# Softmax probabilities copied by a DMA into fp32r buffers before their transposes; seven entries of the ordering list changed

## The chip, the cores and the metric

The kernel runs as one program on one core of a Trainium2 chip. Its engines are TensorE (PE, matrix products and transposes), VectorE (DVE), ScalarE (ACT), GpSimd (POOL) and SyncE (SP), which only issues DMA transfers here. The metric is the device time of one execution in microseconds (us).

## The reference

Clustered attention over 16 heads (2 batches of 8), then two feed-forward blocks. Per head q, k and v are 768x64; the result is 1536x512.

```python
mask = q_assign[:, :, :, None] == k_assign[:, :, None, :]   # argmax over 16 centroids each
scores = np.where(mask, scale * q @ k.T, -1e9)
attn = np.exp(scores - scores.max(-1))
attn = attn / (attn.sum(-1) + 1e-9)
x = (attn @ v)                                # -> (1536, 512)
x = ((x @ w1) * (x @ w2)) @ w3 @ w_out        # first block, d_ff 1024
h = x @ w_in                                  # second block, d_ff 2048
out = (h * np.clip(h + 3, 0, 6) / 6) @ w_out2
```

## The kernel before

Products are made in fp32r, with each operand split into a rounded high part and a remainder (`hi`, `lo`), so that one product is three or four passes. The feed-forward weights come as 64-bit numbers and are made into fp32 by ACT, POOL and DVE (`conv_ops`, lines 665 to 707, tiles raw, cvt, cvs).

One head is worked in six row blocks c of 128 queries. For each block `scores` (L495) makes 128x768 scores into one of two PSUM slots of `pst`; `smax` (L504, DVE) takes the negated row maximum; `sexp` (L512, ACT) writes the exponentials as one fp32 tile p and sums them. Three blocks make a half `hf`. For each of the six key blocks of a half, `p_T` (L520) transposes three 128x128 pieces of the three p tiles into a PSUM tile `ptr`, with the fp32 identity `id_f`; `p_hi` (ACT) copies it rounded into `ph`, `p_lo` (DVE) writes the remainder into `pl`; after two key blocks `av` (L540) multiplies both with v. So there are 32 halves, 192 groups of three transposes, 96 score blocks. The stacked q and k are transposed the same way in `stack_T` (L363), but from fp32r tiles (`qs`, `ks`) with the fp32r identity `id_r`.

While attention runs, PE also does the product w3 @ w_out (`psw`, L771), and later x @ w1 and x @ w2 of the first batch (`psab`, L843). When the last head is done, its memory is opened for the next stage (`open_top`), where `psx` (L956) begins, and from there the second block follows (`psab` L1093, `psh` L1403, `po` L1447).

The order on every engine is fixed before the run. Each step is entered with `op(name, engine, duration, function, needs, due, take, drop, lat)`: `take` and `drop` name rings of buffers of limited number, `lat` is added to the end of a transfer. `Plan.order` (L64) places the steps one after another by these durations, choosing on each engine among those that can start soonest the one with the lowest `due`; in attention one unit of `due` is one score block. Every engine, SP included, then works through its own list in that order and waits at an instruction whose inputs are not there. All transfers are issued by SP. `attn_ops` (L613) enters the steps of a head: S1 and S are the two parts of the scores, mx the maximum, ex the exponential, pT, ph, pl, av the rest. `LT` sets how many units after the first block of a half its transposes are due.

Of the kernel before, what the change touches and what calls it, by code (L numbers as in the profile page):

```python
# [8 lines left out]
F32 = mybir.dt.float32  # L9
# [127 lines left out]
def cluster_attention_moe_kernel(  # L137
# [14 lines left out]
    nc = tc.nc  # L152
# [42 lines left out]
    def blk(i):  # L195
# [14 lines left out]

    NQ, NK, NP, NO = 1, 1, 6, 1
    plan = Plan({
        "raw": 2, "rawx": 6, "cvt": 2, "cvs": 2, "hl": 2, "wT": 3, "m": 1, "s": 3, "r": 2, "a": 1, "x": 1, "x1b": 1,
        "qn": 2, "kn": 2, "vn": 1, "qs": NQ, "ks": NK, "vs": 2, "qB": 2, "kB": 2, "qA": 2, "kA": 2, "oh": NO,
        "p": NP, "ph": 2, "pl": 2, "den": 2, "T": 1, "O": 1, "rdb": 1, "as1": 1, "as2": 1, "asb": 2, "rdr": 1,
        "ga": 1, "gb": 1, "w16": 1, "whl": 1, "gA": 1, "gB": 1, "gv": 2, "t": 6, "h": 1, "gh": 6, "sn": 5, "L": 2, "bL": 2, "bs": 8, "F": 1, "wof": 2,
    })
    op = plan.op  # L220
# [203 lines left out]
    def prep_ops(h):  # L424
# [26 lines left out]
        for hf in range(2):  # L451
# [7 lines left out]
        op(("pa", h), "pe", 1.3, lambda: assign_mm(h), [("CqB", h, 0), ("CqB", h, 1), ("CkB", h, 0), ("CkB", h, 1),  # L459
            ("cTc", 1)] + [("pa", h - 1)] * (h > 0),  # L460
           due=b - 5, take=("s",))
        for n in range(8):
# [7 lines left out]
    def flat(t):  # L470
        return t.rearrange("p a f -> p (a f)")

    pps, dens, psS, phl, avs, Ts, rdb, ptr = {}, {}, {}, {}, {}, {}, {}, {}


    psr = ps_r.tile([128, 2, S], F32, tag="r", name="pst")
# [30 lines left out]

    def sexp(h, c):
        d = dens[h]
        p = at.tile([128, 2, HF], F32, tag="p", name="p", bufs=NP)  # L510
        n = NC * h + c
        done["ex", n] = [other_banks(nc.scalar.activation(  # L512
            out=flat(p), in_=psS.pop((h, c)), func=AF.Exp, bias=d[:, 0, c:c + 1], accum_out=d[:, 1, c:c + 1]
        ), ("S", n + 1))]
        pps[h, c] = flat(p)
# [88 lines left out]
    def pair_lo(e, pr):  # L604
        sub_on(e, xT0[0][:, 1, pr, :], flat(Ts.pop(pr)), xT0[0][:, 0, pr, :])

    LT, LA = 3.4, 1.6

    def attn_ops(h):
        b = NC * h  # L610
        for c in range(NC):
            t = b + c
            nd = [("C" + n, h, f) for n in ("qB", "kB", "k") for f in range(2)] + [("Cq", h, c // 3)]  # L613
            last = c == NC - 1
            prev = [("ex",) + divmod(t - 1, NC)] if t else []
            nd += [("S1",) + divmod(t - 1, NC)] if t else []
            nd += [("ex",) + divmod(t - 2, NC)] if t > 1 else []
            op(("S1", h, c), "pe", 0.43, lambda c=c: scores(h, c, 0), nd, due=t, take=("r",))
            op(("S", h, c), "pe", 0.22, lambda c=c: scores(h, c, 1), [("S1", h, c)] + prev, due=t + 0.1,
               drop=("qB", "kB", "qA", "kA") if last else ())  # L620
# [3 lines left out]
            op(("ex", h, c), "act", 0.88, lambda c=c: sexp(h, c), (("mx", h, c),), due=t + 0.6, take=("p",),  # L624
                drop=("r",))
        for hf in range(2):
            for s in range(3):
                u = b + 3 * hf + s + LT
                for i in range(2):
                    op(("pT", h, hf, s, i), "pe", 0.325, lambda hf=hf, s=s, i=i: p_T(h, hf, s, i),  # L630
                       [("ex", h, 3 * hf + c) for c in range(3)], due=u + 0.2 * i, take=("s",),
                       drop=("p",) * 3 if s == 2 and i == 1 else ())
# [5 lines left out]
                op(("av", h, hf, s), "pe", 0.65, lambda hf=hf, s=s: av(h, hf, s),  # L638
                   [("pl", h, hf, s, 0), ("pl", h, hf, s, 1), ("vlo", h)] + [("av", h, hf, s - 1)] * (s > 0),
                       due=u + LA,  # L640
                   take=("a",) if s == 0 else (), drop=("ph",) + (("vs",) if hf and s == 2 else ()))
# [153 lines left out]
    for hf in range(2):  # L795
        for m in range(J1):
# [9 lines left out]
                drop=("s",))  # L806
            for kk in range(4):
                g, fin = 4 * hf + kk, m == J1 - 1
                op(("w", m, g), "pe", 0.645, lambda m=m, g=g: w_mm(m, g),
                   [("wtl", m, hf), ("wol", g)] + ([("w", m, g - 1)] if kk else [("w", m - 1, 4 * hf + 3)] if m else  # L810
                                                   [("w", J1 - 1, 3)] if hf else []),
                   due=wdue(m, g), take=("m",) if kk == 0 else (),
                   drop=(("wT",) if kk == 3 else ()) + (("hl", ("ga", "gb")[hf]) if fin and kk == 3 else ()) + (
                       ("x1b",) if fin and g == J1 - 1 else ()))
# [45 lines left out]
    for j in range(J1):  # L860
# [9 lines left out]
        for hf in range(2):  # L870
            for w in range(2):
                u = j + (2 * hf + w) / 4
                d = AB0 + AR * u
                for kk in range(KD):
                    op(("ab", j, hf, w, kk), "pe", 0.485, lambda j=j, hf=hf, w=w, kk=kk: ab_mm(j, hf, w, kk),
                       [("abl", j, w), ("xl", kk)] + ([("ab", j, hf, w, kk - 1)] if kk else []),
                       due=d + AR * kk / 16, take=("m",) if kk == 0 else (),
                       drop=("hl",) if hf and w and kk == KD - 1 else ())
# [676 lines left out]
```

## Time and profile before

| | |
|---|---|
| time, median of 3 runs | 786.79 us (786.77 to 787.0) |
| profiled execution, first to last instruction (its span) | 785.5 us; what lies around the span is not in the page: 1.3 us by the median |
| PE busy | 762.6 us (97%) |
| DVE busy | 659.7 us (84%) |
| ACT busy | 534.7 us (68%) |
| POOL busy | 258.2 us (33%) |
| granted TensorE clock | 0.997 of 2.4 GHz, mean |
| DMA moved | 94.24 MB, mean 120 GB/s |

An engine's busy time counts its instructions; a PE instruction is counted until its modelled end, while the next one already starts, so the time that an instruction costs is read from the start of one to the start of the next. The profile names idle time by what ended it. A row is line, engine, operation, tiles, and the count.

### The profile page before, as it was taken

The numbers are of one execution on the slowest core, as the hardware profiler recorded it, in microseconds if no ns is written. First come the engines' busy times: TensorE is split into PE (matmuls) and PEld (weight loads), VectorE is DVE, ScalarE is ACT, GpSimd is POOL, SyncE is SP. The second block draws the span as 40 slices with busy tenths as digits, with TensorE's granted clock in tenths as the row PEclk, the third lists the DMA queues.
The fourth block names the chain that finished last, engine by engine and source line by source line (L and its number), as shares of the span: only waits on it lengthen the run. The fifth ranks groups of instructions, "written<-read, shape, count | busy, mean of one in ns | idle before, by whom it ended". The sixth has DMA issues, their size and how long they took to land.

```text
span 785.5 us, 12835 instructions
## 1 busy us (share of the span) xinstructions
PE 762.6 (97%) x4471; PEld 698.3 (89%) x4471; DVE 659.7 (84%) x1193; ACT 534.7 (68%) x1061; POOL 258.2 (33%) x277
## 2 busy tenths in 40 slices
PE   6799999999999999999999999999999999999997
PEld 5688887789899999999999999989898989888986
DVE  7998898999999897788998798979999976666742
ACT  5679897777877786767763565746776667555543
POOL 5733757344555454323232131611122111010100
PEclk9999999999999999999999999999999999999999
DMA  7443343333454441333344543366533424212102
GB/s 248 131 149 105 89 138 101 109 113 97 120 159 146 114 148 53 90 112 114 106 138 132 152 160 114 109 217 213 164 124 120 138 91 148 81 55 68 41 14 81
DMA packets 57041, 94.24 MB, mean 120 GB/s; under 512 B 5168, under 2 KB 33936, under 8 KB 56976
## 3 DMA queue, kind: packets, MB, share of 16 engines
q1 hardware_dynamic: 56976, 93.43, 38.4%
q8 instruction: 35, 0.57, 0.3%
q14 instruction: 30, 0.25, 0.1%
HBM read 71.34 MB, written 15.78 MB: 111 GB/s over the span
## 4 chain that ended last, share of the span: by engine, by line
PE 83%; DVE 9%; ACT 4%; issue 3%; DMA 1%; ACTq 0%; POOL 0%; DVEq 0%; SPq 0%; POOLq 0%
PE po L1447 17%; PE psh L1403 15%; PE psab L843 8%; PE pst L495 7%; PE av L540 7%; PE psab L1093 7%; PE ptr L520 7%; PE psw L771 5%; PE psx L956 4%; PE pa L389 3%; DVE den L504 1%; DVE pl L184 1%; DVE cvs L720 1%; ACT p L512 1%; PE ptkB L363 1%
## 5 line engine op out<-in xcount | busy, mean ns | idle before, releaser
L711 POOL TENSOR_SCALAR cvt<-cvt 128x512 f32<-128x512 f32 x72 | 75.8, 1056 | 192.6 <-ACT cvt L187 181.2
L187 ACT ACTIVATE ph<-ptr 128x384 fp32r<-128x384 f32 x192 | 91.0, 487 | 44.9 <-PE ptr L520 43.9
L184 DVE TENSOR_TENSOR pl<-ptr,ph 128x384 fp32r<-128x384 f32 x192 | 103.4, 550 | 16.9 <-ACT ph L187 15.3
L504 DVE TENSOR_REDUCE den<-pst 128x1 f32<-128x768 f32 x96 | 91.2, 950 | 8.6 <-PE pst L495 7.0
L512 ACT ACTIVATE p<-pst,den 128x768 f32<-128x768 f32 x96 | 86.3, 898 | 9.8 <-DVE den L504 9.0
L520 PE MATMUL ptr<-id_f,p 128*128 128x128 f32 x576 | 88.4, 274 | 1.7 <-DVE pl L184 1.0
L843 PE MATMUL psab<-xT,abhl 128*128 128x384 f32 x384 | 86.9, 349 | 0.6 <-ACT asb L187 0.6
L520 PEld LDWEIGHTS ptr<-id_f,p 128*128 128x128 f32 x576 | 68.6, 140 | 11.4 <-DVE pl L184 2.3
L495 PE MATMUL pst<-kB,qB 128*128 128x512 f32 x192 | 70.1, 368 | 4.4 <-ACT p L512 4.1
L540 PE MATMUL av<-ph,vs 128*128 128x384 f32 x192 | 69.7, 363 | 0.0
L843 PEld LDWEIGHTS psab<-xT,abhl 128*128 128x128 f32 x384 | 64.4, 189 | 2.9 <-ACT asb L187 1.1
L540 PE MATMUL av<-pl,vs 128*128 128x384 f32 x192 | 65.0, 339 | 0.0
L495 PE MATMUL pst<-kA,qA 128*128 128x512 f32 x192 | 63.9, 338 | 0.2 <-issue 0.2
L187 ACT ACTIVATE m_sn<-psh 128x384 f32<-128x384 f32 x64 | 31.1, 486 | 36.1 <-PE psh L1403 35.9
L1425 ACT ACTIVATE tt<-m_sn,three 128x384 f32<-128x384 f32 x48 | 29.5, 617 | 37.3 <-DVE m_sn L1413 28.2
L724 DVE SCALAR_TENSOR_TENSOR cvs<-cvt,cvs 128x512 int32<-128x512 int32 x72 | 52.4, 731 | 0.2
L771 PE MATMUL psw<-woh,wT 128*128 128x512 f32 x128 | 52.6, 417 | 0.0
L187 ACT ACTIVATE cvt<-raw 128x512 f32<-128x512 f32 x72 | 47.6, 666 | 6.9 <-DVE m_gB L184 3.5
L720 DVE SCALAR_TENSOR_TENSOR cvs<-raw,cvs 128x512 int32<-128x512 int32 x72 | 49.6, 694 | 0.4
L495 PEld LDWEIGHTS pst<-kB,qB 128*128 128x128 f32 x192 | 36.1, 188 | 10.1 <-ACT p L512 7.7
L716 DVE TENSOR_SCALAR cvs<-cvt 128x512 int32<-128x512 int32 x72 | 33.5, 470 | 12.2 <-POOL cvt L711 6.7
L1447 PE MATMUL po<-m_hl,m_gv 128*128 128x512 f32 x162 | 43.7, 393 | 0.0
(203 smaller groups left out, 1948.9 us busy)
## 6 DMA issues: line engine op xcount, KB each, us to landing
raw<-in_moe_w_dram SPq DMA_DIRECT2D x32, 512.0 KB, 3.8
m_gb<-set SPq DMA_DIRECT2D x64, 256.0 KB, 3.2
raw<-in_moe_w_out_dram SPq DMA_DIRECT2D x24, 512.0 KB, 3.9
raw<-in_moe_w_in_dram SPq DMA_DIRECT2D x16, 512.0 KB, 4.0
set<-cvs SPq DMA_DIRECT2D x32, 256.0 KB, 3.8
abp<-cvs SPq DMA_DIRECT2D x16, 256.0 KB, 2.2
b_gv<-abp SPq DMA_DIRECT2D x16, 256.0 KB, 2.8
qn<-in_q_dram SPq DMA_DIRECT2D x16, 192.0 KB, 4.1
```

What stands on the lines that cost most here:

```text
L184: nc.vector.tensor_tensor(out=out, in0=a, in1=b, op=ALU.subtract)
L187: nc.scalar.activation(out=out, in_=in_, func=AF.Copy, **kw)
L495: x = mm(out=psr[:, t, ks_], lhsT=TT["q" + nm, h][:, i, cs_], rhs=flat(TT["k" + nm, h])[:, ks_], start=st, stop=sp)
L504: done["mx", n] = [other_banks(nc.vector.tensor_reduce(out=dens[h][:, 0, c:c + 1], in_=psS[h, c], axis=AX.X, op=ALU.max, negate=True), ("S ...
L512: done["ex", n] = [other_banks(nc.scalar.activation(out=flat(p), in_=psS.pop((h, c)), func=AF.Exp, bias=d[:, 0, c:c + 1], accum_out=d[:, 1 ...
L520: nc.tensor.transpose(pt[:, blk(c)], pps[h, 3 * hf + c][:, blk(2 * s + i)], id_f)
L540: mm(out=t[:, 0:HF], lhsT=vs_t[h][:, 2 * s + i, :], rhs=x_[:, i, :], start=(s == 0 and i == 0 and n == 0), stop=(s == 2 and i == 1 and n = ...
L711: (nc.gpsimd.tensor_scalar if e == "pool" else ts)(out=tf, in0=tf, scalar1=H_MAX, scalar2=-H_MAX, op0=ALU.min, op1=ALU.max)
L771: mm(out=ps, lhsT=wT[m, hf][:, a, blk(kk)], rhs=w_[hf][:, kk, :], start=(kk == 0 and n == 0), stop=(kk == 3 and n == 2))
L843: mm(out=ps[:, 0:HF], lhsT=s[:, w, a, blk(kk)], rhs=xT0[0][:, x_, kk, hf * HF:hf * HF + HF], start=(kk == 0 and n == 0), stop=(kk == KD - ...
L1403: mm(out=ps[:, 0:HF], lhsT=left(p, l, a, kk), rhs=x[:, x_, kk, :], start=(st and kk == 0 and m == 0), stop=(kk == 1 and m == 2), skip_grou ...
L1447: mm(out=outs[b, c], lhsT=g[:, a, blk(c % 3)], rhs=w[:, w_, :], start=(first and a == 0 and w_ == 0), stop=(last and a == 1))
```

## The change

Each p tile is now written under the name `praw` into a ring of three fp32 buffers. A new step `pd` has SP copy it (128 partitions x 3 KB, 384 KB) into an fp32r tile of the old ring `p` of six, bit for bit. The transposes read that tile with `id_r` and write an fp32r PSUM tile, which `p_hi` and `p_lo` read as fp32, as before. They now need the three copies of a half in place of the three exponentials.

```diff
+        "p": NP, "pr": NX, ...                       # NX = 3, NP = 6
...
     def sexp(h, c):
-        p = at.tile([128, 2, HF], F32, tag="p", name="p", bufs=NP)
+        p = praw[h, c] = at.tile([128, 2, HF], F32, tag="pr", name="praw", bufs=NX)
...
+    def p_hop(h, c):
+        t = at.tile([128, 2, HF], F32R, tag="p", name="p", bufs=NP)
+        nc.sync.dma_start(out=t.bitcast(F32), in_=praw.pop((h, c)))
+        pps[h, c] = flat(t)
...
-        pt = ptr[i] = ps_s.tile([128, 512], F32, tag="s", name="ptr")
+        pt = ptr[i] = ps_s.tile([128, 512], F32R, tag="s", name="ptr")
-            nc.tensor.transpose(pt[:, blk(c)], pps[h, 3 * hf + c][:, blk(2 * s + i)], id_f)
-        phl[h, hf, s, i, "t"] = pt
+            nc.tensor.transpose(pt[:, blk(c)], pps[h, 3 * hf + c][:, blk(2 * s + i)], id_r)
+        phl[h, hf, s, i, "t"] = pt.bitcast(F32)
...
-    LT, LA = 3.4, 1.6
+    LT, LA = 4.2, 1.6
...
-            op(("ex", h, c), "act", 0.88, ..., due=t + 0.6, take=("p",), drop=("r",))
+            op(("ex", h, c), "act", 0.88, ..., due=t + 0.6, take=("pr",), drop=("r",))
+            op(("pd", h, c), "dma", 1.3, lambda c=c: p_hop(h, c), (("ex", h, c),), due=t + 0.7, take=("p",),
+                drop=("pr",), lat=2.2)
...
-                    op(("pT", h, hf, s, i), "pe", 0.325, ..., [("ex", h, 3 * hf + c) for c in range(3)], ...)
+                    op(("pT", h, hf, s, i), "pe", 0.18, ..., [("pd", h, 3 * hf + c) for c in range(3)], ...)
...
-                op(("w", m, g), "pe", 0.645, ...)
+                op(("w", m, g), "pe", 0.695, ...)
```

The other entries: `pa` 1.3 to 1.35, `S1` 0.43 to 0.47, `S` 0.22 to 0.238, `av` 0.65 to 0.70, `ab` 0.485 to 0.525. All instructions after L216 stand up to six lines lower.

The lists on the engines change from the first head on. First, PE in the last half of the last head, from its last score product (`pst` 128x256) to the first transposes of that half (`ptr`, three or six in a row). The order before:

```order
L495 MATMUL pst<-kA,qA 128x256
L520 MATMUL ptr<-id_f,p 128x128 x3
L843 MATMUL psab<-xT_1204,abhl 128x384 x6
L520 MATMUL ptr<-id_f,p 128x128 x3
L843 MATMUL psab<-xT_1204,abhl 128x384 x3
L540 MATMUL av<-ph,vs 128x384
L540 MATMUL av<-pl,vs 128x384
L540 MATMUL av<-ph,vs 128x384
L540 MATMUL av<-pl,vs 128x384
L843 MATMUL psab<-xT_1204,abhl 128x384 x3
L520 MATMUL ptr<-id_f,p 128x128 x6
```

Here the earlier `ptr` rows belong to the half before, and the last row is the first of the last half. The order now, from the rows that follow the last score product, a group of three `ptr`, three `psab`, three `ptr` and six `psab`:

```order
L544 MATMUL av<-ph,vs 128x384
L544 MATMUL av<-pl,vs 128x384
L544 MATMUL av<-ph,vs 128x384
L544 MATMUL av<-pl,vs 128x384
L849 MATMUL psab<-xT_1291,abhl 128x384 x3
L524 MATMUL ptr<-id_r,p 128x128 x6
L544 MATMUL av<-ph,vs 128x384
L544 MATMUL av<-pl,vs 128x384
L544 MATMUL av<-ph,vs 128x384
L544 MATMUL av<-pl,vs 128x384
L849 MATMUL psab<-xT_1291,abhl 128x384 x9
L524 MATMUL ptr<-id_r,p 128x128 x3
```

Six more transposes of the half before, a further `av` and six more `psab` now stand ahead of the first transposes of the last half.

Second, SP while the sixth to eighth head runs (`qA`, `kA`: stacked q and k moved to other partitions; `vn`: v of a head; `abp`: converted weights stored; numbers are those of buffers). The order before:

```order
L588 DMA rdb_2567<-rd7_117 64x768
L692 DMA raw_2849<-in_moe_w1_dram 128x4x256
L836 DMA abp0_86<-cvs_2773 128x512
L329 DMA vn_2956<-in_v_dram 128x384
L692 DMA raw_3022<-in_moe_w2_dram 128x4x256
L373 DMA qA_131<-qB_3002 64x768
L836 DMA abp0_86<-cvs_2924 128x512
L373 DMA kA_133<-kB_3039 64x768
```

The order now, from the same `rdb` on:

```order
L592 DMA rdb_2624<-rd7_117 64x768
L698 DMA raw_2937<-in_moe_w1_dram 128x4x256
L518 DMA p_2968<-praw_2950 128x768
L518 DMA p_3006<-praw_2992 128x768
L842 DMA abp0_86<-cvs_2858 128x512
L329 DMA vn_3062<-in_v_dram 128x384
L518 DMA p_3079<-praw_3053 128x768
L518 DMA p_3123<-praw_3100 128x768
L373 DMA qA_131<-qB_3098 64x768
L373 DMA kA_133<-kB_3121 64x768
L698 DMA raw_3173<-in_moe_w2_dram 128x4x256
L518 DMA p_3194<-praw_3153 128x768
```

The copies stand between the loads and stores, each behind whatever the row above it waits for.

Third, PE at the end of attention, up to the first `psx`. The order before:

```order
L520 MATMUL ptr<-id_f,p 128x128 x6
L843 MATMUL psab<-xT_1204,abhl 128x384 x3
L540 MATMUL av<-ph,vs 128x384
L540 MATMUL av<-pl,vs 128x384
L540 MATMUL av<-ph,vs 128x384
L540 MATMUL av<-pl,vs 128x384
L540 MATMUL av<-ph,vs 128x384
L540 MATMUL av<-pl,vs 128x384
L540 MATMUL av<-ph,vs 128x384
L540 MATMUL av<-pl,vs 128x384
L843 MATMUL psab<-xT_1204,abhl 128x384 x24
L956 MATMUL psx_5427<-gh_5389,Whl 128x384 x18
```

And now:

```order
L524 MATMUL ptr<-id_r,p 128x128 x6
L544 MATMUL av<-ph,vs 128x384
L544 MATMUL av<-pl,vs 128x384
L544 MATMUL av<-ph,vs 128x384
L544 MATMUL av<-pl,vs 128x384
L849 MATMUL psab<-xT_1291,abhl 128x384 x12
L544 MATMUL av<-ph,vs 128x384
L544 MATMUL av<-pl,vs 128x384
L544 MATMUL av<-ph,vs 128x384
L544 MATMUL av<-pl,vs 128x384
L849 MATMUL psab<-xT_1291,abhl 128x384 x12
L962 MATMUL psx_5611<-gh_5586,Whl 128x384 x18
```

Twelve `psab` moved from behind the last `av` to before it; twelve are left between the last `av` and the first `psx`.

## Rows read from the trace of the kernel before

**Rows 1.** The page: the chain that ended last, shares of the span by line.

```profile
PE po L1447 17%; PE psh L1403 15%; PE psab L843 8%; PE pst L495 7%; PE av L540 7%; PE psab L1093 7%; PE ptr L520 7%; PE psw L771 5%; PE psx L956 4%; PE pa L389 3%; DVE den L504 1%; DVE pl L184 1%; DVE cvs L720 1%; ACT p L512 1%; PE ptkB L363 1%
```

**Rows 2.** Busy time by stretch: length, PE, PEld, DVE, ACT, POOL, clock, DMA, GB/s.

```profile
40.00:400.00 360.00, 354.55 (x2355) 323.33 (x2354) 323.75 (x609) 282.78 (x610) 161.73 (x182) 1.00 0.39 117
160.00:240.00 80.00, 78.84 (x529) 70.67 (x528) 76.71 (x147) 64.50 (x140) 37.88 (x44) 1.00 0.40 119
```

**Rows 3.** Groups by line and shape: busy us, mean ns, idle before.

```profile
L520 PE MATMUL ptr<-id_f,p 128*128 128x128 f32 x576 | 88.4, 274 | 1.7 <-DVE pl L184 1.0 <-ACT qA L187 0.2
...
L363 PE MATMUL ptkB<-id_r,ks 128*128 128x128 f32 x96 | 13.1, 249 | 0.1
```

**Rows 4.** Timeline of PE around both kinds of transposes: start, length.

```profile
228.79 0.37 PE L363 MATMUL ptqB<-id_r,qs 128*128 128x128 f32 x3
229.00 1.28 PE L843 MATMUL psab<-xT,abhl 128*128 128x384 f32 x6
230.12 0.28 PE L495 MATMUL pst<-kB,qB 128*128 128x256 f32 x1
230.23 0.28 PE L495 MATMUL pst<-kA,qA 128*128 128x256 f32 x1
230.35 0.82 PE L520 MATMUL ptr<-id_f,p 128*128 128x128 f32 x6
230.93 0.42 PE L540 MATMUL av<-ph,vs 128*128 128x384 f32 x1
231.19 0.33 PE L540 MATMUL av<-pl,vs 128*128 128x384 f32 x1
231.36 0.34 PE L540 MATMUL av<-ph,vs 128*128 128x384 f32 x1
...
231.71 0.40 PE L495 MATMUL pst<-kB,qB 128*128 128x512 f32 x1
231.94 0.40 PE L495 MATMUL pst<-kA,qA 128*128 128x512 f32 x1
```

**Rows 5.** Timeline: third block of one half, scores to transposes.

```profile
249.78 0.28 PE L495 MATMUL pst<-kA,qA 128*128 128x256 f32 x1
...
251.47 0.90 ACT L512 ACTIVATE p<-pst,den 128x768 f32<-128x768 f32 x1
...
253.42 0.49 PE L520 MATMUL ptr<-id_f,p 128*128 128x128 f32 x3
```

**Rows 6.** Timeline: the same of the last half of the last head.

```profile
380.40 0.28 PE L495 MATMUL pst<-kA,qA 128*128 128x256 f32 x1
...
383.00 0.89 ACT L512 ACTIVATE p<-pst,den 128x768 f32<-128x768 f32 x1
...
383.99 0.82 PE L520 MATMUL ptr<-id_f,p 128*128 128x128 f32 x6
```

**Rows 7.** Line 373, 192 KB between SBUF tiles: issue to landing.

```profile
DMA to landing us min/median/max: 2.6/2.8/4.8
```

**Rows 8.** Line 692, 512 KB loads: issue to landing.

```profile
DMA to landing us min/median/max: 3.3/3.9/8.3
```

**Rows 9.** The page's DMA queue over the span.

```profile
q1 hardware_dynamic: 56976, 93.43, 38.4%
```

**Rows 10.** What SP's queue waited for, 20 to 400 us: total, times, longest.

```profile
SPq L692 <- DVE cvs L720: 83.4, 31, 7.8
SPq L329 <- POOL vs L181: 64.7, 13, 9.0
```

**Rows 11.** Timeline: last products of attention, and psx.

```profile
394.43 0.44 PE L540 MATMUL av<-pl,vs 128*128 128x384 f32 x1
394.89 2.38 PE L843 MATMUL psab<-xT,abhl 128*128 128x384 f32 x12
...
397.85 2.35 PE L843 MATMUL psab<-xT,abhl 128*128 128x384 f32 x12 [0.58 <-ACT asb L187]
...
400.04 4.15 PE L956 MATMUL psx<-gh,Whl 128*128 128x384 f32 x23
```

More of the change, by code (lines that the diff above doesn't have):

```diff
@@ L206, in cluster_attention_moe_kernel @@
     rd_dram = [tc.dram_tile([NC, 128], F32, name=f"rd{h}") for h in range(NH)]
-    NQ, NK, NP, NO = 1, 1, 6, 1
+    NQ, NK, NP, NO, NX = 1, 1, 6, 1, 3
     plan = Plan({
@@ L216, in cluster_attention_moe_kernel @@
         "qn": 2, "kn": 2, "vn": 1, "qs": NQ, "ks": NK, "vs": 2, "qB": 2, "kB": 2, "qA": 2, "kA": 2, "oh": NO,
-        "p": NP, "ph": 2, "pl": 2, "den": 2, "T": 1, "O": 1, "rdb": 1, "as1": 1, "as2": 1, "asb": 2, "rdr": 1,
+        "p": NP, "pr": NX, "ph": 2, "pl": 2, "den": 2, "T": 1, "O": 1, "rdb": 1, "as1": 1, "as2": 1, "asb": 2, "rdr": 1,
         "ga": 1, "gb": 1, "w16": 1, "whl": 1, "gA": 1, "gB": 1, "gv": 2, "t": 6, "h": 1, "gh": 6, "sn": 5, "L": 2, "bL": 2, "bs": 8, "F": 1, "wof": 2,
@@ L458, in prep_ops @@
                 (("Ck", h, hf), ("Dq", h)), due=dd + 0.06, drop=("s",))
-        op(("pa", h), "pe", 1.3, lambda: assign_mm(h), [("CqB", h, 0), ("CqB", h, 1), ("CkB", h, 0), ("CkB", h, 1),
+        op(("pa", h), "pe", 1.35, lambda: assign_mm(h), [("CqB", h, 0), ("CqB", h, 1), ("CkB", h, 0), ("CkB", h, 1),
             ("cTc", 1)] + [("pa", h - 1)] * (h > 0),
@@ L471, in flat @@
         return t.rearrange("p a f -> p (a f)")
-    pps, dens, psS, phl, avs, Ts, rdb, ptr = {}, {}, {}, {}, {}, {}, {}, {}
+    praw, pps, dens, psS, phl, avs, Ts, rdb, ptr = {}, {}, {}, {}, {}, {}, {}, {}, {}
     psr = ps_r.tile([128, 2, S], F32, tag="r", name="pst")
@@ L617, in attn_ops @@
             nd += [("ex",) + divmod(t - 2, NC)] if t > 1 else []
-            op(("S1", h, c), "pe", 0.43, lambda c=c: scores(h, c, 0), nd, due=t, take=("r",))
-            op(("S", h, c), "pe", 0.22, lambda c=c: scores(h, c, 1), [("S1", h, c)] + prev, due=t + 0.1,
+            op(("S1", h, c), "pe", 0.47, lambda c=c: scores(h, c, 0), nd, due=t, take=("r",))
+            op(("S", h, c), "pe", 0.238, lambda c=c: scores(h, c, 1), [("S1", h, c)] + prev, due=t + 0.1,
                drop=("qB", "kB", "qA", "kA") if last else ())
@@ L623, in attn_ops @@
                take=("den",) if c == 0 else ())
-            op(("ex", h, c), "act", 0.88, lambda c=c: sexp(h, c), (("mx", h, c),), due=t + 0.6, take=("p",),
+            op(("ex", h, c), "act", 0.88, lambda c=c: sexp(h, c), (("mx", h, c),), due=t + 0.6, take=("pr",),
                 drop=("r",))
+            op(("pd", h, c), "dma", 1.3, lambda c=c: p_hop(h, c), (("ex", h, c),), due=t + 0.7, take=("p",),
+                drop=("pr",), lat=2.2)
         for hf in range(2):
@@ L629, in attn_ops @@
                 for i in range(2):
-                    op(("pT", h, hf, s, i), "pe", 0.325, lambda hf=hf, s=s, i=i: p_T(h, hf, s, i),
-                       [("ex", h, 3 * hf + c) for c in range(3)], due=u + 0.2 * i, take=("s",),
+                    op(("pT", h, hf, s, i), "pe", 0.18, lambda hf=hf, s=s, i=i: p_T(h, hf, s, i),
+                       [("pd", h, 3 * hf + c) for c in range(3)], due=u + 0.2 * i, take=("s",),
                        drop=("p",) * 3 if s == 2 and i == 1 else ())
@@ L637, in attn_ops @@
                        (("ph", h, hf, s, i),), due=u + 0.2 * i + 0.2, drop=("s",))
-                op(("av", h, hf, s), "pe", 0.65, lambda hf=hf, s=s: av(h, hf, s),
+                op(("av", h, hf, s), "pe", 0.70, lambda hf=hf, s=s: av(h, hf, s),
                    [("pl", h, hf, s, 0), ("pl", h, hf, s, 1), ("vlo", h)] + [("av", h, hf, s - 1)] * (s > 0),
@@ L808, in cluster_attention_moe_kernel @@
                 g, fin = 4 * hf + kk, m == J1 - 1
-                op(("w", m, g), "pe", 0.645, lambda m=m, g=g: w_mm(m, g),
+                op(("w", m, g), "pe", 0.695, lambda m=m, g=g: w_mm(m, g),
                    [("wtl", m, hf), ("wol", g)] + ([("w", m, g - 1)] if kk else [("w", m - 1, 4 * hf + 3)] if m else
@@ L874, in cluster_attention_moe_kernel @@
                 for kk in range(KD):
-                    op(("ab", j, hf, w, kk), "pe", 0.485, lambda j=j, hf=hf, w=w, kk=kk: ab_mm(j, hf, w, kk),
+                    op(("ab", j, hf, w, kk), "pe", 0.525, lambda j=j, hf=hf, w=w, kk=kk: ab_mm(j, hf, w, kk),
                        [("abl", j, w), ("xl", kk)] + ([("ab", j, hf, w, kk - 1)] if kk else []),
```

1 line of the change is left out of this document (removed).

## Prediction

> **What bounds the kernel now.** I read the chain that ended last first: the reader is to see that nearly all its large shares are TensorE lines, those of attention (pst, av, ptr, psab L843, psw, pa) and those after it, while VectorE and ScalarE come in with one per cent a line [rows 1]. Then the busy time by stretch. Between 40 and 400 us, where the changed steps run, TensorE is busy 354.55 of 360 us and VectorE 323.75; in the tightest part, 160 to 240, they are busy 78.84 and 76.71 of 80 [rows 2]. So TensorE bounds attention, and VectorE stands so close behind it that it can take over. The stages after 400 start from the end of attention, through psx [rows 11]; what attention gains or loses therefore moves the end by about as much. Last I read the timeline for what an operation costs from start to start, since the durations of TensorE overlap.
>
> **What the transposes give.** In the group view the 576 fp32 transposes take 88.4 us of TensorE, 0.153 each; the fp32r transposes of the stacked k, same shape and same kind of operands as the new ones, take 13.1 for 96, 0.136 each [rows 3]. By that the change saves 576 x 0.017 = 9.8 us. The timeline gives a second value [rows 4]. Six fp32 transposes start at 230.35 and the next product at 230.93, 0.58; that product then runs 0.26 to the next start where its like takes 0.17 (231.19 to 231.36), so 0.09 more of the cost lies on it: 0.67 for six, 0.335 for three. Three fp32r transposes take 0.21 (228.79 to 229.00), and the six products behind them 1.12, which is 0.1 over six at 0.17: 0.29 to 0.31 for three. The saving by this is about 0.04 a group, 192 x 0.04 = 7.7 us. I take the middle, 0.045 a group, 8.6 us. The list's own step, 0.325 to 0.18, would be 0.145 x 192 = 27.8 us, and nothing in the trace bears the 0.18 out.
>
> It matters here that fp32 is not slow in this place. A product of 512 columns takes 0.23 from start to start (231.71 to 231.94), one fp32 transpose of 128 columns 0.58/6 = 0.097 [rows 4]; four passes over 128 columns would have cost about the former. The Trainium skill (TensorE: Matmul & The Clock Gate, Terms) says that a load or product carries a transpose mode that is four times faster for fp32; by that rule the fast form is already in use before the change and little is left to gain. The trace agrees: 0.097 against 0.07. Read without that rule, as fp32 at a quarter of the rate, the change would be worth 576 x (0.23 - 0.07) = 92 us, which the trace rules out, since the whole group takes 88.4.
>
> **What the copy costs.** 96 copies of 384 KB are added, issued by SP. The trace has no such transfer. Its neighbours on both sides are the 192 KB moves between SBUF tiles, which land 2.6 us after their issue at best and 2.8 in the median, and the 512 KB loads, 3.3 and 3.9 [rows 7, 8]. By size 384 KB stands at 0.6 between them: 3.0 at best, 3.5 in the median. The ends for the range are 2.6 and 4.8, the longest of the 192 KB moves. The bytes: 93.43 MB took 38.4% of the span on the 16 engines [rows 9], so 37.7 MB more take 122 us of all of them, and the share in attention goes from 0.39 to about 0.7. The DMA engines stay below full, but a copy will meet a load in front of it more often than a load does now. I take 3.7 us.
>
> What does it collide with? The wait of the transposes moves from the exponential to the copy. From the start of a third block's last score product to the end of its exponential the trace shows 2.6 us in one half (249.78 to 252.37) and 3.5 in the last (380.40 to 383.89); TensorE had 3.6 us of other work in between in both (253.42 and 383.99 are the first transposes), which left 1.05 and 0.10 [rows 5, 6]. This work is what covers the copy. In the new order, for the last half, it is 12 transposes, 21 products psab, 8 av and the score product: 4 x 0.295 + 21 x 0.175 + 8 x 0.17 + 0.12 = 6.3 us, 2.7 more than before. I added up the rows of all 32 halves so, at 0.17 to 0.19 for a product of 384 columns, 0.23 for 512, 0.11 for 256 and 0.1 for a transpose [rows 4]: the cover grows by 3.5 us in the median, to 7.7, with some six halves at 5 to 6.4. Against a copy of 3.7 the typical half keeps its margin, and the short ones are late: the last by 3.5 + 3.7 - 6.3 = 0.9 us, with the shorter exponential path of [rows 5] nothing. I put 4 to 5 us on all short halves together: six at about 0.7. Behind a late transpose stand, on TensorE, the av products and the next scores, for which VectorE (mx) and ScalarE (ex) wait. The bounds are 0 (copies at 3.0) and, with copies at 4.8, about 23 us by the same covers and a mean path of 3.2.
>
> The Trainium skill (DMA: Bandwidth & Descriptors, Anatomy of one DMA) puts a transfer at about 2.0 us fixed plus its bytes at 436 GB/s; an estimate by that page is 2.0 + 0.9 = 2.9 us for a copy. The fit is for another way of issuing, and the 192 KB moves at 2.8 [rows 7] are above the 2.5 that it gives for them. By it no half would be late and the sum would be the whole 8.6 us.
>
> **The queue.** SP works in order. Before, it stood 64.7 us at loads of q, k and v until GpSimd had freed a buffer, 9.0 at the longest, and 83.4 at weight loads until VectorE had [rows 10]. Nothing urgent stood behind them. Now copies do: in the second order a load of v stands ahead of two copies. Each list is drawn up with these waits in it, so I add nothing of its own for it, but it is where the landing time can grow beyond 4 us.
>
> **Other edits.** praw has three buffers and a block comes each 3.8 us (96 in some 360), so a buffer is free long before ScalarE wants it: nothing. The copies, the maxima and the remainders on VectorE stay the same in number and size: nothing. The six raised durations remove no instruction; the list gets nearer the trace for products, and further off for the transposes (0.18 for what costs 0.295, 192 x 0.115 = 22 us too little). I take nothing for the reordering, with 3 us on either side. At the end of attention 24 psab (4.7 us) covered what lies between the last av and psx, with 0.58 us of waiting in it (394.89 to 400.04) [rows 11]; now 12 do, 2.1 us. The path there is a PSUM copy, a copy of the gate and a subtraction; before, the first psx could start 5.2 us after, and a stall of up to 1 us may come in place of the 0.58: I add 0.4.
>
> **Sum.** 8.6 saved, less 4.3 for late copies and 0.4 at the end: 3.9 us. On the profiled span of 785.5 that is 781.6; the median of the runs is 1.3 above the span, so 782.9.
>
> **The rivals.** First, the copies come late and it is slower. The mechanism is the copy for the third block of each half, held by SP's order or by a load in front. It decides from the point where late halves cost 8.6 us, by the covers above at a landing of about 4.1 us; at 4.5, 14 us are lost and the time is 786.8 + 5.4 = 792, at 4.8 it is 801. For it: the margin of 0.10 [rows 6], a DMA share going to 0.7, loads that took up to 8.3 us [rows 8]. Against: the median of everything near in size is below 4, and most halves have more cover than need.
>
> Second, VectorE takes the gain. It is busy 96% between 160 and 240 [rows 2], its work in attention is not less, and what TensorE saves turns into waits for pl and mx. Time 786 to 787. Against: over 40 to 400 it has 36 us idle, four times the saving.
>
> Third, the list is right about 0.18: 27.8 us off TensorE. VectorE's 36 us of idle would then be nearly used up, and I give it half, 773. Against it stand all of [rows 3, 4].
>
> **Chances.** Forecast 0.52, with a range of its own of 778 to 786; late copies 0.27; VectorE 0.16; the cheap transposes 0.05. The time is 782.9. The range for 8 in 10 goes from 775 (part of the third case, reordering in our favour) to 797 (most of the first). What measurement can tell here is about 0.2%, 1.6 us. Faster by more: 0.54, from the forecast less its upper edge, the third case, and a little of the second. Within: 0.18. Slower: 0.28, the first case and a little of the second.
>
> **What would show it.** In the profile after: fp32r transposes at about 0.21 for three from start to start and near 78 us for the 576; copies landing at 3.5 to 4 us; TensorE's idle time ahead of ptr, now 1.7 us, at some 5 with the DMA p<-praw named; the first psx near 396 and the same distance from there to the end. Copies at 4.5 or more with tens of us of waiting ahead of ptr would prove the first rival; no such wait and psx still at 400, the second; transposes at 0.18 or less with their follower, the third.

## Result and profile after

The changed kernel takes 798.31 us (median of 4 runs, 797.01 to 801.13), the kernel before beside it 786.89: the ratio is 1.0135, 95% interval 1.0112 to 1.0158. It is 11.4 us slower; 3.9 us faster was forecast. The profiled execution has a span of 799.3 us, 13.8 above that of before; it is the longest of the four, 801.13.

Busy time by stretch of the changed kernel (columns: the stretch, its length, busy us and count of TensorE, of its weight loads, of VectorE, ScalarE and GpSimd, then the granted clock, the DMA share and GB/s). The second and third row answer to [rows 2]; the first runs from 20 us to the first psx:

```profile
core 0: us, PE busy (x) PEld busy (x) DVE busy (x) ACT busy (x) POOL busy (x), PEclk, DMA share, GB/s
20.00:412.56 392.56, 370.74 (x2446) 332.33 (x2445) 344.83 (x632) 294.78 (x634) 176.19 (x203) 0.98 0.62 206
40.00:400.00 360.00, 344.82 (x2292) 310.19 (x2291) 318.13 (x588) 275.36 (x595) 156.94 (x183) 0.98 0.63 210
160.00:240.00 80.00, 76.69 (x522) 66.34 (x522) 72.67 (x137) 62.04 (x136) 36.06 (x43) 1.00 0.61 203
95.00:100.00 5.00, 3.78 (x18) 3.20 (x19) 4.51 (x5) 2.05 (x5) 4.45 (x4) 0.73 0.63 182
100.00:105.00 5.00, 5.00 (x23) 4.50 (x24) 2.31 (x6) 2.35 (x5) 1.79 (x3) 0.58 0.42 130
145.00:150.00 5.00, 5.00 (x22) 4.71 (x22) 4.42 (x7) 0.87 (x2) 4.02 (x5) 0.51 0.64 192
150.00:155.00 5.00, 4.25 (x25) 3.69 (x25) 4.10 (x9) 3.41 (x8) 0.80 (x2) 0.81 0.42 141
```

The stretch from 20 us to the first psx in the kernel before:

```profile
20.00:400.04 380.04, 370.61 (x2444) 335.43 (x2443) 342.16 (x636) 295.69 (x637) 177.60 (x201) 1.00 0.40 118
```

The two first rows hold the result. The same work up to psx takes 392.56 us instead of 380.04. TensorE's idle time went from 9.4 to 21.8 (length less busy). Its busy time did not fall, though the transposes became cheaper: the granted clock was below 1.0 in some stretches, down to about 0.5, its 1.2 GHz level. Counted in stretches of 5 us as (1 - clock) x 5, that is 8.5 us of full-speed work; 370.74 - 8.5 = 362.2 is 8.4 below before. VectorE and ScalarE had hardly more to do than before (344.83 and 294.78 against 342.16 and 295.69). They and TensorE waited for each other.

Where the time goes is read from the start of one step in both traces: the exponentials of the 7th, the 37th and the last of the 96 blocks, before and now.

```profile
47.30 0.91 ACT L512 ACTIVATE p<-pst,den 128x768 f32<-128x768 f32 x1
156.15 0.91 ACT L512 ACTIVATE p<-pst,den 128x768 f32<-128x768 f32 x1
383.00 0.89 ACT L512 ACTIVATE p<-pst,den 128x768 f32<-128x768 f32 x1
```

```profile
48.01 0.90 ACT L512 ACTIVATE praw<-pst,den 128x768 f32<-128x768 f32 x1 [1.18 <-issue]
171.07 0.90 ACT L512 ACTIVATE praw<-pst,den 128x768 f32<-128x768 f32 x1
395.30 0.92 ACT L512 ACTIVATE praw<-pst,den 128x768 f32<-128x768 f32 x1
```

The changed kernel is 0.7 us late at the 7th block, 14.9 at the 37th and 12.3 at the last. The whole loss arises between some 50 and 170 us; from there to the end of attention, where the cheaper transposes count as well, a little of it comes back.

The transposes themselves, as a group and on TensorE's timeline (start, duration, then the instruction), which answer to [rows 3, 4]:

```profile
L524 PE MATMUL ptr<-id_r,p 128*128 128x128 f32 x576 | 71.6, 243 | 4.2 <-DVE pl L184 2.8 <-ACT qA L187 0.6 <-DVE as L404 0.3
```

```profile
85.79 0.63 PE L524 MATMUL ptr<-id_r,p 128*128 128x128 f32 x6
86.26 0.47 PE L495 MATMUL pst<-kB,qB 128*128 128x512 f32 x1
86.57 0.39 PE L495 MATMUL pst<-kA,qA 128*128 128x512 f32 x1
86.80 0.37 PE L524 MATMUL ptr<-id_r,p 128*128 128x128 f32 x3
87.01 0.46 PE L777 MATMUL psw<-woh,wT 128*128 128x512 f32 x1
```

Three start in 0.21 us (86.80 to 87.01), six in 0.47. What the transposes and their weight loads, all on one line of the kernel, waited for (us, times, both added up):

```profile
  DVE pl L184: 6.8, 10
  ACT qA L187: 2.1, 5
  issue: 1.1, 2
  DVE as L404: 1.1, 3
  DMA p<-praw: 0.8, 2
```

The copy is the last entry: 0.8 us in the whole kernel, 0.3 of it ahead of a transpose and 0.5 ahead of a weight load. The waits that grew name VectorE and ScalarE; TensorE's idle time from 20 to 410 us by what ended it (us in total, times, longest):

```profile
PE pst L495 <- ACT praw L512: 6.4, 11, 1.4
PE ptr L524 <- DVE pl L184: 2.8, 4, 1.5
PE pto L378 <- ACT qA L187: 1.4, 2, 1.2
PE pa L389 <- DVE kB L229: 1.3, 2, 1.1
PE av L544 <- ACT T L187: 1.2, 2, 0.9
```

One of the places, while the fourth head runs: TensorE, then VectorE and GpSimd at the same time.

```profile
94.99 0.45 PE L363 MATMUL ptkB<-id_r,ks 128*128 128x128 f32 x3 [0.61 <-DVE pl L184]
95.55 0.39 PE L495 MATMUL pst<-kB,qB 128*128 128x256 f32 x1
95.78 0.28 PE L495 MATMUL pst<-kA,qA 128*128 128x256 f32 x1
95.90 0.39 PE L495 MATMUL pst<-kB,qB 128*128 128x512 f32 x1
96.13 0.40 PE L495 MATMUL pst<-kA,qA 128*128 128x512 f32 x1
97.64 1.46 PE L389 MATMUL pa<-cT,qB 128*128 128x32 f32 x6 [1.12 <-DVE kB L229]
```

```profile
94.39 0.55 DVE L184 TENSOR_TENSOR pl<-ptr,ph 128x384 fp32r<-128x384 f32 x1
94.85 2.27 DVE L730 SCALAR_TENSOR_TENSOR cvs<-cvt,cvs 128x512 int32<-128x512 int32 x1
97.04 0.55 DVE L229 CAST kB<-ptkB 128x384 fp32r<-128x384 f32 x1
```

```profile
94.75 1.83 POOL L181 TENSOR_TENSOR xT<-T,xT 128x768 fp32r<-128x768 f32 x1
```

The cast of kB stands on VectorE behind a weight conversion of 2.27 us, which ran beside a GpSimd subtraction (the median of its kind is 0.68); the products pa wait 1.12 us until it is done, with nothing else ahead of them in TensorE's list, and then run at the low clock. None of these waits is of a kind that the change added; what changed is which instruction stands where.

### The profile page after: what moved, and what is told of

It is laid out like the page before. It is cut to its first block, busy times and chain, and to the rows that moved or that the text cites. A ratio compares the mean times of both kernels' runs of the same rounds, so it can differ in the third digit from the quotient of the medians.

```text
span 799.3 us, 13154 instructions
## 1 busy us (share of the span) xinstructions
PE 764.4 (96%) x4471; PEld 694.9 (87%) x4471; DVE 667.0 (83%) x1194; ACT 535.3 (67%) x1060; POOL 256.9 (32%) x277
## 4 chain that ended last, share of the span: by engine, by line
PE 75%; DVE 9%; ACT 6%; issue 2%; DMA 2%; POOL 0%; DVEq 0%; ACTq 0%
PE po L1453 17%; PE psh L1409 15%; PE psx L962 8%; PE psab L1099 7%; PE psab L849 6%; PE av L544 6%; PE pst L495 5%; PE psw L777 4%; PE ptr L524 3%; PE pa L389 2%; ACT praw L512 2%; DVE den L504 2%; DVE pl L184 2%; ACT ph L187 1%; DVE cvs L726 1%
## 5 line engine op out<-in xcount | busy, mean ns | idle before, releaser
L717 POOL TENSOR_SCALAR cvt<-cvt 128x512 f32<-128x512 f32 x72 | 78.8, 1095 | 201.4 <-ACT cvt L187 183.9
L512 ACT ACTIVATE praw<-pst,den 128x768 f32<-128x768 f32 x96 | 86.2, 898 | 15.0 <-DVE den L504 12.3
L524 PEld LDWEIGHTS ptr<-id_r,p 128*128 128x128 f32 x576 | 64.5, 142 | 13.8 <-DVE pl L184 4.0
L524 PE MATMUL ptr<-id_r,p 128*128 128x128 f32 x576 | 71.6, 243 | 4.2 <-DVE pl L184 2.8
L726 DVE SCALAR_TENSOR_TENSOR cvs<-raw,cvs 128x512 int32<-128x512 int32 x72 | 54.4, 759 | 0.6
L722 DVE TENSOR_SCALAR cvs<-cvt 128x512 int32<-128x512 int32 x72 | 35.3, 495 | 11.8 <-POOL cvt L717 6.2
```

The lines of the kernel that those rows point to most:

```text
L512: done["ex", n] = [other_banks(nc.scalar.activation(out=flat(p), in_=psS.pop((h, c)), func=AF.Exp, bias=d[:, 0, c:c + 1], accum_out=d[:, 1 ...
L717: (nc.gpsimd.tensor_scalar if e == "pool" else ts)(out=tf, in0=tf, scalar1=H_MAX, scalar2=-H_MAX, op0=ALU.min, op1=ALU.max)
```

## Experiments

Each time is given with its difference to the kernel before, run beside it on the same chip.

**The raised durations alone.** The six durations that were raised, in the kernel before:

```diff
-S1 0.43, S 0.22, pa 1.3, av 0.65, w 0.645, ab 0.485
+S1 0.47, S 0.238, pa 1.35, av 0.70, w 0.695, ab 0.525
```

> The kernel before with the six raised durations alone: no copy, fp32 transposes. Theory O (the list that the raised durations give starves TensorE between 60 and 170 us, whatever the copy does): 794 to 800 us, with the granted clock falling below 1.0 there. Rival C (the copy or its place in SP's queue costs the time): 784 to 789 us, clock 1.0 throughout attention.

788.03 us, +1.2 (ratio 1.0016, 0.9998 to 1.0034), clock 0.997. By themselves they cost no more than the interval; what theory O expected, 794 to 800, did not come.

**The changed kernel with these six back:**

```diff
-S1 0.47, S 0.238, pa 1.35, av 0.70, w 0.695, ab 0.525
+S1 0.43, S 0.22, pa 1.3, av 0.65, w 0.645, ab 0.485
```

> The changed kernel with the six durations as they were, the copy kept. Theory O: back to 780 to 788 us. Rival C: 796 to 802 us, as the changed kernel.

789.21 us, +2.4 (1.0028, 1.0011 to 1.0044). 9.0 us of the 11.4 go away, and so do the falls of the clock at 95 and 145 us; the time lies just above the 780 to 788 of theory O. So the same six numbers that cost 1.2 us in the old list cost 9 in the new one.

**The new lists without the copy**, transposes in fp32 again:

```diff
-        p = praw[h, c] = at.tile([128, 2, HF], F32, tag="pr", ...)
+        p = praw[h, c] = at.tile([128, 2, HF], F32, tag="p", ...)      # ring of 9
-        nc.sync.dma_start(out=t.bitcast(F32), in_=praw.pop((h, c)))
+        pps[h, c] = flat(praw.pop((h, c)))
```

> The lists of the changed kernel on PE, ACT, DVE and POOL, but no copies: ScalarE writes p into a ring of nine and the fp32 transposes read it directly; SP has 96 rows fewer. Theory O: still 797 to 806 us (as slow, and the transposes 8 us dearer where they are not hidden), the psx start near 412 us. Rival C: 785 to 790 us, the psx start near 400.

807.61 us, +20.8. No copy is left, and it is 9.4 us slower than with it. The same lists with fp32r transposes and no copy, further down, take 799.27 us, +11.0; so 9.9 us of this are the dearer transposes, and the order is the loss.

**The old lists with fp32r transposes and no copy** (ScalarE writes the probabilities rounded to fp32r; their low part is left out):

```diff
-        p = at.tile([128, 2, HF], F32, tag="p", name="p", bufs=NP)
+        p = at.tile([128, 2, HF], F32R, tag="p", name="p", bufs=NP)
```

> The lists of the kernel before, no copies; ScalarE writes p rounded to fp32r (the low part of the probabilities is left out) and the transposes are fp32r. It measures the transposes' gain by itself. If it is the 8.6 us of the prediction: 777 to 780 us. If VectorE takes the gain: 784 to 787 us.

779.51 us, -7.3 (0.9919, 0.9902 to 0.9936): the transposes' gain by itself. Up to psx:

```profile
20.00:393.72 373.72, 361.60 (x2445) 325.58 (x2446) 340.19 (x638) 295.56 (x638) 177.82 (x201) 1.00 0.39 119
```

TensorE is busy 9.0 us less than before, and its idle time is 12.1. This kernel is faster than both, at the price of the low part.

**The transposes at the price that the trace shows**, otherwise as changed:

```diff
-                    op(("pT", h, hf, s, i), "pe", 0.18, ...)
+                    op(("pT", h, hf, s, i), "pe", 0.295, ...)
```

> The changed kernel with one number put back towards the trace: a group of three transposes stands in the ordering list at 0.295 us instead of 0.18. Price theory: the loss of the new order comes from this entry, 192 x 0.115 = 22 us of TensorE that the list does not count, so that TensorE's work is laid out too early against VectorE's and ScalarE's; with it right the time is 781 to 788 and the granted clock does not fall. Lead-time rival (the loss comes from LT, 3.4 raised to 4.2, with the copy step): 794 to 800, the clock still falls. If both share it: near 791.

791.60 us, +4.2: 7.2 of the 11.4 go, clock 0.998. That lies between the two theories. Either group of numbers put back repairs most of it; the 7.2 and the 9.0 overlap, since together they are more than the 11.4.

**The lead time back:**

```diff
-    LT, LA = 4.2, 1.6
+    LT, LA = 3.4, 1.6
```

> The changed kernel with LT, the due time of a half's transposes behind its exponentials, put back from 4.2 to 3.4. Lead-time rival: 781 to 788, clock at 1.0. Price theory: 794 to 803, since the copies have less cover and the list's error stays. If both share it: near 791.

815.36 us, +27.9, 12 us above what the price theory gave as well. With the copies in the list the longer lead is needed; the lead-time rival falls.

**The copy without room**, in the old order on every engine:

```diff
+        t = at.tile([128, 2, HF], F32R, tag="p", name="p", bufs=NP)
+        nc.sync.dma_start(out=t.bitcast(F32), in_=p)          # right behind the exponential
```

> The order of the kernel before on every engine, with the copy issued by SP right behind each exponential and the transposes reading the copy: what the copy costs where the order leaves no room for it. By the covers of the prediction (1.05 us and 0.10 us left ahead of the first transpose of a half) a copy of some 3 us makes TensorE wait 1.5 to 3 us in each of 32 halves, 48 to 96 us, less 7.3 for the cheaper transposes: 825 to 875, with the wait put down to DMA p<-praw. If the wait is taken up elsewhere, as in the changed kernel, 785 to 800.

859.18 us, +71.8. Its transposes from 20 to 410 us (busy, mean, idle time ahead by what ended it):

```profile
L522 PE MATMUL ptr<-id_r,p 128*128 128x128 f32 x498 | 67.6, 249 | 50.6 <-DMA p<-praw 48.7 <-DVE pl L184 1.5 <-DVE wT L184 0.3
```

Here the copy is named, 48.7 us. This is what [rows 5, 6] were about; the changed kernel's order does hide it.

**More products ahead of the clock's falls**, in `scores`:

```diff
+        if not part and (15 <= n < 20 or 29 <= n < 34):
+            for _ in range(2):
+                x = mm(out=psr[:, t, ks_], lhsT=TT["qB", h][:, i, cs_], rhs=flat(TT["kB", h])[:, ks_], ...)
```

> The changed kernel with the 512-column score product of high parts done two more times in blocks 15 to 19 and 29 to 33, ahead of the two places where the granted clock fell; 20 products at 0.23, 4.6 us at most where TensorE sets the pace. Clock theory: with TensorE busier there the granted clock stays at 1.0 and 8.8 us come back: 790 to 795. Rival (the clock is only a sign, VectorE and ScalarE set the pace there): 798 to 803, whatever the clock does.

802.67 us, +15.2, and the clock fell in the stretches from 95 to 105 us and from 145 us all the same: it tells nothing of what the fall costs.

**Products right ahead of pa**, meant to fill the wait there:

```diff
+        if h in (4, 6):
+            for c in range(2 * h):
+                mm(out=pa.rearrange("p a b c -> p (a b c)"), lhsT=TT["qB", h][:, 0, 0:128],
+                   rhs=TT["qB", h][:, c % 2, :], start=True, stop=True)
```

> The changed kernel with products on qB (384 columns, their result overwritten) put ahead of the assignment products pa of heads 4 and 6, 8 and 12 of them: there TensorE waits for VectorE's kB right ahead of the two places where the granted clock fell. 20 x 0.18 = 3.6 us, 1.1 to 1.5 of it inside the waits. Clock theory: without the wait the clock stays at 1.0 in 80 to 160 us, the 8.4 us that it cost come back, and the time is 791 to 794. Rival (the clock is a sign, the others set the pace): the clock stays up and the time is 798 to 802 all the same. If the clock falls in the same places, nothing is told.

800.65 us, +13.2. The products did not come to lie in the wait: they waited for the same cast of kB, and pa came behind them.

```profile
95.89 1.66 PE L388 MATMUL pa<-qB 128*128 128x384 f32 x8 [1.11 <-DVE kB L229]
97.40 0.73 PE L393 MATMUL pa<-cT,qB 128*128 128x32 f32 x6
```

So they add 1.5 us of TensorE's time there (95.89 to 97.40) and 2.2 in the other place, 3.7 together. The wait of 1.11 us is as long as the 1.12 in the changed kernel, yet the two falls of the clock are gone; a shorter one comes later:

```profile
95.00:100.00 5.00, 4.11 (x29) 3.97 (x30) 3.92 (x9) 1.49 (x3) 2.72 (x3) 1.00 0.41 115
145.00:150.00 5.00, 4.44 (x30) 3.72 (x29) 5.00 (x10) 3.11 (x7) 0.46 (x1) 1.00 0.44 144
160.00:165.00 5.00, 3.72 (x20) 2.88 (x21) 3.46 (x6) 4.23 (x10) 2.11 (x3) 0.74 0.41 137
```

What did the clock give back? There are two readings, and they differ. By the medians, 798.31 + 3.7 - 800.65 = 1.4 us, for a mean clock of 0.991 in the changed kernel's four executions and 0.996 in these (the middle of each), which is 4 us of full-speed work. By the two profiled executions, up to psx, 412.56 + 3.7 - 411.05 = 5.2 us, where (1 - clock) x 5 falls from 8.5 to 1.8, by 6.8 us. Both take the added products at their full cost.

The executions of one and the same kernel also say that it is not nothing: over the 207 whose clock is on record, each compared only with its own kernel on the same chip, a mean clock lower by 0.01 goes with 5.2 us more, two thirds of the 7.9 that this is at full speed. Whether the low clock made them longer, or the waits that went ahead of it, these figures do not tell. So the clock theory in its full form (791 to 794) falls, and the clock's price in the changed kernel stays open: between 1.4 us and, as an estimate, two thirds of the difference in clock to the kernel before (0.991 against 0.998, 5.5 us), 3.7.

**A longer lead**, in the kernel with 0.295:

```diff
-    LT, LA = 4.2, 1.6
+    LT, LA = 4.6, 1.6
```

> The changed kernel with the transposes at 0.295 us in the list and LT at 4.6 instead of 4.2. If the 4 us that the run with 0.295 alone is above the kernel before are a shortage of lead, 785 to 789; if they are not, 790 to 795.

796.82 us, +9.4. More lead is not what is missing. Both ranges were missed: it is 5 us slower than the same with 4.2 (+4.2), so with the raised durations a small step in the list moves the time by 5 us.

**Room alone:** the changed kernel with every TensorE duration as before.

```diff
-pT 0.18, S1 0.47, S 0.238, pa 1.35, av 0.70, w 0.695, ab 0.525
+pT 0.325, S1 0.43, S 0.22, pa 1.3, av 0.65, w 0.645, ab 0.485
```

> The copy, the fp32r transposes, the copy's step in the list and LT 4.2, with every TensorE duration of the list as before the change (0.325 for the transposes too). Price theory: the loss comes from the numbers, and making room for the copy costs next to nothing: TensorE idle to the first psx 10 to 13 us, clock at 1.0, time 779 to 783. Room rival: a list with the copy's step and the longer lead starves TensorE whatever the prices: idle 16 us or more, 787 to 792.

789.89 us, +2.4 (1.0027, 1.0009 to 1.0046). The price theory wanted 779 to 783; with the transposes' 7.3 taken off, this list still loses 9.7. Four kernels with the same copy and the same lead of 4.2 can now be put side by side:

| transposes in the list | the six other durations | against before |
|---|---|---|
| 0.325 | as before | +2.4 |
| 0.18 | as before | +2.4 |
| 0.295 | raised | +4.2 |
| 0.18 | raised | +11.4 |

The low price of the transposes costs nothing while the six others are as before, though that list counts the least TensorE time of the four. It costs 7.2 us only together with the raised ones. So the loss does not follow from how far a list undercounts TensorE.

The copies of the room-alone kernel, in the view of issues (KB each, median us to landing):

```profile
p<-praw SPq DMA_DIRECT2D x96, 384.0 KB, 2.9
```

**Unread copies in the old order**, first of the newest block, then of the block two before:

```diff
+        x = at.tile([128, 2, HF], F32, tag="pr", name="praw", bufs=3)
+        nc.sync.dma_start(out=x, in_=p.bitcast(F32))       # then: in_=pps[divmod(n - 2, NC)]
```

> The old order with fp32r transposes (ScalarE writes the probabilities rounded, their low part is left out, as in the run without a copy at 779.5), and the 96 copies issued behind the exponentials into buffers that nobody reads: what the transfers and SP's waits cost by themselves. If they cost nothing, 778 to 781. If traffic (37.7 MB) or SP, held at the exponentials ahead of its loads, slows the rest, 783 to 790.

> The old order with fp32r transposes of rounded probabilities, and unread copies as before, but each of the block two before, so that SP does not wait for an exponential. Queue theory (SP held at the exponentials makes the weight loads late): 778 to 782, ScalarE's wait for raw gone. Traffic theory (37.7 MB more slow the loads and the engines): 786 to 791 as with copies of the newest block.

789.52 us, +2.1, and 785.77, -2.6 (0.9975, 0.9962 to 0.9989): 9.4 and 4.7 above the same order without them. ScalarE's waits in the first, and below them its wait for raw in the run without copies:

```profile
ACT p L512 <- DVE den L504: 10.8, 20, 1.7
ACT cvt L187 <- DMA raw<-in_moe_w_dram: 10.1, 7, 2.3
```

```profile
ACT cvt L187 <- DMA raw<-in_moe_w_dram: 1.1, 1, 1.1
```

In the second that wait is 4.9 us; its time lies between the ranges of the two theories. The wait grew by 9.0 and 3.8 us, about what the two lost. So copies that stand in SP's queue without a place in the list delay the weight loads behind them, half of it by SP's waiting for the exponential; what the other half is, queue or traffic, was not separated.

**The copies taken out of the two new lists**, the changed kernel's and the room alone's (rounded probabilities, low part left out):

```diff
-        p = praw[h, c] = at.tile([128, 2, HF], F32, tag="pr", ...)
+        p = praw[h, c] = at.tile([128, 2, HF], F32R, tag="p", ...)     # ring of 9
-        nc.sync.dma_start(out=t.bitcast(F32), in_=praw.pop((h, c)))
+        pps[h, c] = flat(praw.pop((h, c)))
```

> The changed kernel's lists without the copies, the transposes still in fp32r (ScalarE writes the probabilities rounded, their low part is left out). If the lists alone carry the loss: 796 to 800, as with the copies. If the copies carry 8 to 10 us of it, as in the old order: 787 to 791.

> The lists with room for the copy at the old prices (789.9 with copies), without the copies, transposes in fp32r, low part left out. If the room costs the 10 us that this kernel is above the old order with the same transposes (779.5): 787 to 791. If the copies and SP's waits do: 778 to 782.

799.27 us, +11.0, and 788.93, +0.6 (1.0011, 0.9997 to 1.0025). With the copies it was +11.4 and +2.4. So where the list has a place for them, 96 copies cost 0.5 and 1.8 us, which is no more than the intervals of these ratios (1.5 to 2 us on either side). Up to psx the two are, first the changed kernel's lists, then the room alone's:

```profile
20.00:409.68 389.68, 367.79 (x2445) 329.51 (x2445) 344.39 (x631) 294.99 (x634) 176.75 (x203) 0.99 0.36 110
```

```profile
20.00:400.08 380.08, 364.52 (x2445) 326.02 (x2445) 344.65 (x627) 295.53 (x638) 179.86 (x204) 1.00 0.38 113
```

**The copies on ScalarE's queue**, in the room-alone kernel:

```diff
-        nc.sync.dma_start(out=t.bitcast(F32), in_=praw.pop((h, c)))
+        nc.scalar.dma_start(out=t.bitcast(F32), in_=praw.pop((h, c)))
```

> The lists with room for the copy at the old prices, the copies issued by ScalarE instead of SP. If SP's order holds up loads there: 780 to 785, faster than both kernels. If it is the room in the list: 787 to 791. If ScalarE's own work is held up by the issues (it then waits for a free p buffer): 792 or more.

795.81 us, +7.5: worse than SP's queue by 5. The range for ScalarE's work held up was 792 or more; that this is the reason was not shown.

**Room made in two other ways**, from the room-alone kernel:

```diff
-    LT, LA = 4.2, 1.6
+    LT, LA = 4.4, 1.6          # then 4.6, with pT 0.295 in place of 0.325
```

> The copy with the old prices and LT 4.4 instead of 4.2. If the room as such costs the 9.4 us, 787 to 792 as with 4.2. If it is the one list that came out, neighbours scatter: 780 to 800, not within 2 us of each other.

> The copy with LT 4.6, the transposes at 0.295 and the other TensorE durations as before the change. If the room as such costs the 9.4 us, 787 to 792. If lists scatter, anything from 780 to 800; under 785 it beats both kernels.

788.25 us, +1.3, and 788.48, +1.5. With 4.2 it was +2.4. All three lose 8.5 to 9.7 us against the old order with the same transposes (-7.3), and so does the changed kernel with the six durations back (+2.4): among lists with the old durations it is the room, not one unlucky list. Room is here the copy's step, its rings and the longer lead together; no run took them apart.

## Why the prediction was wrong

The sum of the runs, each against its own kernel before: transposes -7.3 (old order, rounded), room for the copy +7.9 (to +0.6), the new prices +10.3 (to +11.0), the copies +0.5: 11.4. Each time against its own kernel before has an interval of some 1 to 2 us on either side.

**The transposes: right.** 8.6 us were worked out; TensorE's busy time fell by 9.0 in the old order, the time by 7.3. The group is now 71.6 us where 78 was expected, and three take 0.21. So the fp32 transposes were not slow before: read as fp32 at a quarter of the rate they would have given 92. The Trainium skill (TensorE: Matmul & The Clock Gate, Terms) states a transpose mode that is four times faster for fp32; the small gain agrees with the transposes having been in it.

**The copies: right in kind, too dear in size.** 3.7 us landing and 4.3 of late halves were taken; 2.9 was the median in the room-alone run (the changed kernel's trace has no landing times for them), and 0.8 us the waiting. The estimate by the Trainium skill's figures (DMA: Bandwidth & Descriptors, Anatomy of one DMA), 2.9, was met. The first rival's times, 792 to 801, hold the result, but by luck: its mechanism did not happen, no late copy makes the loss.

**SP's queue: right.** "Each list is drawn up with these waits in it, so I add nothing of its own for it": +0.5 in the changed lists. Copies without a place in the list cost 4.7 to 9.4.

**The reordering: the step that failed.** "I take nothing for the reordering, with 3 us on either side." The lists alone cost 18.2 us (+11.0 against -7.3, both without copies). This term was put at nothing without a row for it. The prediction had two signs of it in hand. It saw that the list undercounts the transposes by 22 us and that six durations were raised, and priced neither; the runs show that neither costs much alone (+1.2 for the six in the old list, nothing for 0.18 beside the old six), and that together they cost 9 to 10. And it measured the room only as cover for the copy [rows 5, 6], not what is moved away to make it: 7.9 us without the copies, and 8.5 to 9.7 with them, whichever way it is made.

Why these lists are slower stays open; where they are is on the traces. Without copies and with the same transposes, the changed kernel's lists run 13.5 us behind the old order at the 37th block's exponential, 16.7 at the 61st and 15.7 at the last; the room alone's 2.2, 5.5 and 6.1. So the tight stretch of [rows 2], VectorE busy 76.71 us of 80 from 160 to 240, which lies between the first two of these, costs both some 3 us, and what the new prices cost they cost ahead of it. The second rival named VectorE, but with its amount of work, which would have stopped at no gain.

One candidate was looked at: VectorE's instructions that ran more than 0.1 us over the median of their operation and shape, what they took above it summed up to 400 us. It is 12.5 to 13.6 us in the kernels whose lists have no room for the copy (12.8 before) and 15.7 to 25.1 in those that have it. But it does not rank the latter: 23.8 in the room alone (+2.4), 21.6 in the changed kernel (+11.4) and in its lists without copies (+11.0), 15.7 with 0.295 (+4.2). The same holds for ScalarE's exponentials waiting for VectorE's maxima, in the room alone without copies:

```profile
ACT p L512 <- DVE den L504: 28.8, 36, 1.8
```

in the old order with the same transposes:

```profile
ACT p L512 <- DVE den L504: 10.6, 19, 1.7
```

and in the changed kernel, which is 10 us slower than the first:

```profile
ACT praw L512 <- DVE den L504: 12.3, 17, 1.7
```

So the first figure tells lists with room from those without, but neither goes with the loss, and they are not shown to be the cause. No run moved GpSimd's instructions away from VectorE's alone, and none took the room or the six durations apart.

**The clock** was not in the prediction. It fell behind TensorE's waits and made the busy time look unchanged. Its own price, 1.4 to some 4 us of the 11.4, is within what the lists lost and was not separated from them.

**The end: right in place, too small.** A stall in place of the 0.58 us was foreseen, 0.4 added. It came one product behind the first psx:

```profile
412.56 0.34 PE L962 MATMUL psx<-gh,Whl 128*128 128x384 f32 x1
414.38 0.80 PE L962 MATMUL psx<-gh,Whl 128*128 128x384 f32 x3 [1.48 <-DVE gh L184]
```

That is 0.9 us more than before. From the first psx to the end of the span it is 386.7 us, 385.5 before.

## What to carry to other kernels

When a change alters the numbers by which a list is drawn up, the new list is a part of the change with its own price: run the new order without the new operation, and the new operation in the old order, before either is believed. Here making room for the transfers cost some 8 us and the transfers themselves 0.5 to 1.8. Two groups of numbers that each cost little alone cost 9 to 10 us together, so entries of such a list are to be tried together as well as one by one. A transfer that never shows as a wait is no proof that it was free to place.

## What the runs showed of the hardware

- A VectorE conversion of 128x512 took 2.27 us where its median is 0.68, with a GpSimd subtraction of 1.83 us beside it from 94.75.
- The granted clock went to about 0.5 (1.2 GHz) from 97 to 104 us in the changed kernel. TensorE had been busy 3.72 of the 5 us from 90 to 95, then waited 1.12 us ahead of pa, whose six products of 32 columns took 1.30 us to the next start (97.64 to 98.94). In the run with added products the same wait, 1.11 us, was followed by eight products of 384 columns; the clock stayed at 1.00, and the six took 0.58 (97.40 to 97.98).
- 384 KB between two SBUF tiles landed in 2.9 us by the median of the room alone's 96, within 380 us, with the DMA share at 0.64 there; they cost 1.8 us in it. In the changed kernel the share was 0.62 instead of 0.40 and they cost 0.5 us.
- The same copies issued by ScalarE cost 5 us more than issued by SP (+7.5 against +2.4).
